# LayerNorm of the first four tiles by ScalarE's square root, x0 loaded in two halves, later loads reordered, and the last tile cut into 512 and 128 columns

## The chip, the cores and the metric

The kernel runs on one core of one Trainium2 chip. The metric is the device time of one execution in microseconds (us). The core has five engines with instruction streams of their own: TensorE (PE; its weight loads are shown apart as PEld), VectorE (DVE), ScalarE (ACT), GpSimd (POOL) and SyncE (SP). ScalarE, GpSimd and SyncE also issue DMAs, each into a queue of its own, and 16 DMA engines carry them all.

## The reference

The input x has 2048 rows of 640 numbers. It is normalized per row, and two branches of the normalized rows are added to x: a sliding, dilated local attention with 32 heads of 20 columns and 8 positions, and a bilinear gated unit.

```python
def _layernorm(x, axis=-1, eps=1e-5):
    m = jnp.mean(x, axis=axis, keepdims=True)
    v = jnp.var(x, axis=axis, keepdims=True)
    return (x - m) / jnp.sqrt(v + eps)

def _A_ref(x, wqkv, wo):          # H = 32, Dh = 20, W, dil = 8, 2
    qkv = (x @ wqkv).reshape(B, S, 3, H, Dh).transpose(2, 0, 3, 1, 4)
    idx = pos[:, None] - (jnp.arange(W) * dil)[None, :]
    ...
    logits = jnp.einsum("bhsd,bhswd->bhsw", q, kg) * scale   # -1e9 where idx < 0
    o = jnp.einsum("bhsw,bhswd->bhsd", softmax(logits), vg)
    return o.transpose(0, 2, 1, 3).reshape(B, S, D) @ wo

def _B_ref(x, w_gate, w_up, w_down):     # F = 1536
    return ((x @ w_gate) * (x @ w_up)) @ w_down

xn = _layernorm(x)
return x + _A_ref(xn, A_wqkv, A_wo) + _B_ref(xn, B_w_gate, B_w_up, B_w_down)
```

All inputs and the output are bfloat16.

## The kernel before

The 2048 rows are 16 tiles of 128 rows (t = 0 to 15), four tiles to a chunk of 512 rows (c = 0 to 3). For a tile the kernel loads x (line 166), takes its statistics in two halves of 320 columns (L251), joins them to mean and variance (L257), adds eps (L259), raises to the power -0.5 on GpSimd (L265), and subtracts and multiplies in place (L270). The normalized tile is transposed into xnT, in tiles 0 to 3 by TensorE against an identity (L345), three blocks of 128 columns and then two, each with a copy out of PSUM (L351); from tile 4 on by a DMA transpose issued on SP (L339). TensorE then makes, by chunk, q and k (L407), by tile v in two halves of 320 columns (L440), the logits from VectorE's products of q and shifted k (L478, L488), gate and up (L614), and by tile the down projection together with the attention's output projection, into one PSUM group of 320 columns at a time (L652, L655). VectorE adds x (L661), and the tile is stored (L683; the last two tiles from SP). v goes through a DRAM buffer vD (L461), from which the shifted rows are gathered.

The order of the instructions is a planner's. Each piece of work is a `Step` with an engine, a cost, a shorter time for which it holds the engine (`occ`), and the steps that it needs. `Plan.order` gives every step a latest time (`late`, from its successors) and then plays the engines forward in time, taking on each engine, of the steps that are ready, the one with the earliest `late`. The engines run the instructions in the order so found; the chip's semaphores then decide when each one starts. What is fixed by hand: `inline` chains VectorE's steps of the first tiles one behind another, `pe_main` chains TensorE's main stream and makes it wait for one of six PSUM banks, `load` chains the loads of SP's queue and gives each an assumed landing (`floor`), and `behind(s, a)` makes step s come after step a.

At the start ScalarE's queue issues the two halves of wv (after VectorE's memset of one of its elements, L192) and then loads the table for Exp with a dummy activation (L177); SP's queue issues x0 to x3, then wq (behind a like memset), x4, wk, and x5 to x7 as tiles 0 to 2 have been transposed, since x has five buffers. TensorE runs ten matmuls on zeros (L242) before the first transposes, so that its clock is up. Tile 0 is normalized in two pieces, 384 and 256 columns, and the second copy of its transposes is VectorE's; the others are ScalarE's.

Of the kernel before, what the change touches and what calls it, by code (L numbers as in the profile page):

```python
# [31 lines left out]
class Plan:  # L32
# [15 lines left out]
    def order(self):  # L48
        for s in self.steps:
            s.left = len(s.deps)  # L50
            for d in s.deps:
                d.succ.append(s)
        for s in reversed(self.steps):
            s.late = min([t.late for t in s.succ], default=0.0) - s.cost
        for s in self.steps:
            if s.urgent:
                s.late = -1e6 + s.idx
        free = {}
        queue = {}
        ready = {}  # L60
        for s in self.steps:
            if s.left == 0:
                ready.setdefault(s.eng, []).append((0.0, s))
        out = []
        while True:
            best = None
            for eng, items in ready.items():
                if not items:
                    continue
                f = free.get(eng, 0.0)  # L70
                t0 = max(f, min(r for r, _ in items))
# [12 lines left out]
            out.append(s)  # L84
            for t in s.succ:
                t.left -= 1
                if t.left == 0:
                    at = max(
                        d.start + d.occ if d in t.after else (d.start + d.occ if d.eng == t.eng and d.eng in self.INORDER else d.end + (0.0 if d.eng == t.eng else self.LAG) + t.margin)
                        for d in t.deps  # L90
                    )
                    ready.setdefault(t.eng, []).append((at, t))
        assert len(out) == len(self.steps)
        return out
# [3 lines left out]
def kernel(  # L98
# [11 lines left out]
    nc = tc.nc  # L110
# [35 lines left out]
    wd = const.tile([P, FT, D], BF, name="wd")  # L146
    ident = const.tile([P, P], BF, name="ident")
    mhalf = const.tile([P, 1], F32, name="mhalf")
    Ek = const.tile([P, KT, H], BF, name="Ek")
    negm = const.tile([P, 2, HALO], F32, name="negm")  # L150
    vD = dram.tile([HALO + S, D], BF, name="vD")
# [11 lines left out]
    def load_x(t, eng=None):  # L163
# [2 lines left out]
            (eng or nc.sync).dma_start(out=x[:], in_=x_flat[t * P : (t + 1) * P, :])  # L166
        return fn

    X = {}

    def wload(dst, src, eng=None):
        return lambda: (eng or nc.sync).dma_start(out=dst[:], in_=src.rearrange("(i p) f -> p i f", p=P))

    def table():
        dm = sb.tile([P, 1], F32, name="dm", tag="dm")
        nc.vector.memset(dm[:], 0.0)
        nc.scalar.activation(dm[:], dm[:], ACT.Exp)  # L177

    chain = [None]
    WL = {}  # L180
# [10 lines left out]
    def hold(dst):  # L191
        return lambda: nc.vector.memset(dst[0:1, 0, 0:2], 0.0)  # L192

    X[0] = load(3.0, load_x(0))
    X[1] = load(3.8, load_x(1))
    X[2] = load(4.9, load_x(2))
    X[3] = load(5.3, load_x(3))

    def consts0():
        wz = new("wz", [P, CS], BF, "gs", 3)  # L200
        nc.vector.memset(wz[:], 0.0)  # L201
        hold(wv)()
        nc.vector.memset(mhalf[:], -0.5)
        make_identity(nc, ident[:])

    def consts_e():
# [26 lines left out]
    C0 = add("POOL", 0.6, consts0)  # L233
    WV = [add("ACT", 4.6, part(0), [C0], occ=0.45)]
    WV.append(add("ACT", 5.6, part(1), occ=0.45, after=[WV[0]]))
    TB = add("ACT", 1.6, table, after=[WV[1]])
    CZ = add("POOL", 3.0, consts_z, [C0], occ=1.2)

    def warm():
        ps = psum.tile([P, 512], F32, name="ps", tag="ps", bufs=6)  # L240
        for _ in range(10):
            nc.tensor.matmul(ps[:], lhsT=T["wz"][:, 0:P], rhs=T["wz"][:], start=True, stop=True)  # L242

    main = add("PE", 4.4, warm, [C0])


    def ln_stats(t, g):
# [6 lines left out]
    def ln_aggr(t):  # L254
        def fn():
            mv = new(("mv", t), [P, nc.vector.BN_AGGR_DIM], F32, "mv", 6)
            nc.vector.bn_aggr(mv[:], T["st", t][:])  # L257
            ve = new(("ve", t), [P, 1], F32, "ve", 6)
            nc.vector.tensor_scalar(ve[:], mv[:, 1:2], scalar1=EPS, scalar2=None, op0=ALU.add)  # L259
        return fn  # L260
# [17 lines left out]
    def behind(s, a):  # L278
        s.after.append(a)
        s.deps.append(a)  # L280
        plan.steps.remove(s)
        plan.steps.append(s)

    def inline(eng, cost, fn, deps=(), occ=None):
        s = line[eng] = add(eng, cost, fn, deps, occ=occ, after=[line.get(eng)])
        return s

    def st_in(t, g, d=None):
        return inline("DVE", 0.48, ln_stats(t, g), [d or X[t]], 0.395)

    def aggr_in(t, d):
        GL[t] = inline("DVE", 0.39, ln_aggr(t), [d], 0.35)
        RS[t] = add("POOL", 0.56, ln_rstd(t), [GL[t]])

    def apply_in(t):
        XT[t] = inline("DVE", 0.443, ln_apply(t), [RS[t]], 0.4)
# [24 lines left out]
    def transposes(t):  # L321
# [19 lines left out]
        def half(g0, g1, n):  # L341
            def pe():
                ps = new(("pst", t, n), [P, KT, P], BF, "ps", 6, psum)
                for g in range(g0, g1):
                    nc.tensor.transpose(ps[:, g, :], T["x", t][:, g * P : (g + 1) * P], ident[:])  # L345

            def ev():
                if n == 0:
                    slot()
                o, i = T["xnT", c][:, g0:g1, q * P : (q + 1) * P], T["pst", t, n][:, g0:g1, :]  # L350
                nc.scalar.copy(o, i) if t or n == 0 else nc.vector.tensor_copy(o, i)  # L351
            return pe, ev

        if t < CH:
# [3 lines left out]
            TX[t] = add("ACT", 0.5, ea, [a], occ=0.42)  # L358
            ring.append(TX[t])
            a = pe_main(0.11, pb, [XT[t]])  # L360
            if t:
                TT[t] = add("ACT", 0.42, eb, [a, TX[t]], occ=0.33)
                behind(VE[t - 1][0], TT[t])
            else:
                TT[t] = inline("DVE", 0.4, eb, [a], 0.33)
            ring.append(TT[t])
        elif t < XDMA:
            a = pe_main(0.28, pe, [XT[t]])
# [5 lines left out]
            else:  # L374
                a = TT[t] = add("SP", 2.8, dma, [XT[t], GP.get(c - 2)], occ=1.28, kb=200)
        if t + 5 < W:
            X[t + 5] = load(11.9 + 0.45 * t, load_x(t + 5), [a])
        elif t == 3:
            X[t + 5] = add("ACT", 6.0, load_x(t + 5, nc.scalar), [a], occ=0.45)
        elif 8 <= t < NT - 5:  # L380
# [136 lines left out]
    def softmax(c, hf):  # L517
# [13 lines left out]
        def ex():  # L531
            nc.scalar.activation(T["d", n][:], T["d", n][:], ACT.Exp, scale=scale)

        e = add("ACT", 0.635, ex, [DD[n]], occ=0.54)
        e.margin = 0.8

        def nrm():
# [104 lines left out]
    def down(t):  # L642
        c, q = divmod(t, CH)
        load_xr(t)
        evs = []
        def pe(n, f0, f1, wo_part):
            if f0 == 0:
                new(("psD", t, n), [P, 512], F32, "ps", 6, psum)
            ps = T["psD", t, n]
            sl = slice(n * NS, (n + 1) * NS)  # L650
            for f in range(f0, f1):
                nc.tensor.matmul(ps[:, 0:NS], lhsT=T["hT", c, f][:, q * P : (q + 1) * P], rhs=wd[:, f, sl],  # L652
                                 start=(f == 0), stop=(f == FT - 1 and not wo_part))
            for g in range(KT if wo_part else 0):
                nc.tensor.matmul(ps[:, 0:NS], lhsT=T["oT", t][:, g, :], rhs=wo[:, g, sl],  # L655
                                 start=False, stop=(g == KT - 1 and f1 == FT))

        def evict(n, a):
            def ev():
                sl = slice(n * NS, (n + 1) * NS)  # L660
                nc.vector.tensor_tensor(T["xr", t][:, sl], T["psD", t, n][:, 0:NS], T["xr", t][:, sl], ALU.add)  # L661
            e = add("DVE", 0.486, ev, [a, XR[t]], occ=0.4)
            ring.append(e)
            evs.append(e)

# [9 lines left out]
            a = ends[1]  # L675
        else:
            for n in range(2):
                a = pe_main((FT + KT) * 0.136, lambda n=n: pe(n, 0, FT, True), [*hs, *W2])
                evict(n, a)
        DT[t] = a  # L680

        def st():
            (nc.sync if t >= NT - 2 else nc.gpsimd).dma_start(out=out_flat[t * P : (t + 1) * P, :], in_=T["xr", t][:])  # L683

        OB[t] = add("SP" if t >= NT - 2 else "POOL", 2.3, st, evs, occ=0.5)


    a = st_in(0, 0)
    a = st_in(0, 1, a)
    HQ = inline("DVE", 0.08, hold(wq))  # L690
    aggr_in(0, a)
    WQ = load(8.8, wload(wq, A_wqkv[:, 0:D]), [HQ])
    X[4] = load(9.2, load_x(4))
    WK = load(11.4, wload(wk, A_wqkv[:, D : 2 * D]))
    a = st_in(1, 0)
    a = st_in(1, 1, a)
    XT[0, 0] = inline("DVE", 0.31, ln_apply(0, 0, 3 * P), [RS[0]], 0.25)
    XT[0, 1] = inline("DVE", 0.26, ln_apply(0, 3 * P, D), [RS[0]], 0.2)
    XT[0] = XT[0, 1]
    aggr_in(1, a)  # L700
    halo(0)
    transposes(0)
    vproj(0, (0,))
    a = st_in(2, 0)
    apply_in(1)
    transposes(1)
    a = st_in(2, 1, a)
    aggr_in(2, a)
    vproj(0, (1,))
    vproj(1, (0,))  # L710
    a = st_in(3, 0)
    a = st_in(3, 1, a)
    apply_in(2)
    transposes(2)
    aggr_in(3, a)
    behind(VS[0], RS[3])
    vproj(1, (1,))
    vproj(2, (0,))
    apply_in(3)
    transposes(3)  # L720
    vproj(2, (1,))
# [7 lines left out]
        X[t] = load(30.0, load_x(t), [TT[t - 5]])  # L729
    WL["u"] = load(36.0, wload(wu, B_w_up))  # L730
    qk(0, 0, CS)
    vproj(3)

    def between(c, work):
# [66 lines left out]
```

## Time and profile before

| what | value |
|---|---|
| time, median of 3 runs | 266.16 us (266.08 to 266.64) |
| the profiled execution: its time, its span | 266.25 us, 264.5 us |
| busy: PE, DVE, ACT, POOL | 98%, 81%, 40%, 15% of the span |
| first and last matmul of the span | 1.27 us, 260.88 us |
| loads: 160 KB for a tile of x, 400 KB for half of wv, 800 KB for wq and for wk | |

The span is the time from the first to the last instruction in the profile; the execution's own time lies around it. In the order of time a row shows the start, the duration, the engine, the line, the operation, the tiles written and read, the shapes, how many instructions are merged (x10), and in brackets the idle time before with what ended it. A row with a "q" behind the engine (SPq) is the issue of a DMA. In a table of windows each engine's busy time stands with its number of instructions in the order PE, PEld, DVE, ACT, POOL, and then the granted clock, the busy share of the DMA engines, and GB/s. Durations of matmuls are pipelined: of several in a row, the pitch from start to start is what each one costs.

### The profile page before, as it was taken

How to read it: one execution, taken by the hardware profiler on the slowest of the kernel's cores; microseconds unless marked ns; L12 is line 12 of the kernel's file. 1: busy time of each engine (PE TensorE's matmuls, PEld its weight loads, DVE VectorE, ACT ScalarE, POOL GpSimd, SP SyncE). 2: the span in 40 equal slices, each digit the busy share in tenths (PEclk: the TensorE clock that was granted, in tenths of full speed). 3: DMA queues.
4: the chain of work that ended last, by engine and by line, in shares of the span. 5: the costliest groups of instructions: out<-in, count | busy, mean ns of one | idle time of the engine just before them, and what ended most of it. 6: DMA issues, size and time to landing. Idle time of an engine off the chain costs nothing.

```text
span 264.5 us, 4077 instructions
## 1 busy us (share of the span) xinstructions
PE 258.5 (98%) x1556; PEld 140.8 (53%) x1574; DVE 215.5 (81%) x338; ACT 106.5 (40%) x196; POOL 40.7 (15%) x84
## 2 busy tenths in 40 slices
PE   7999999999999999999999999999999999999994
PEld 2645445444676546444466754644447764445773
DVE  5785998999999999999994799999938999951221
ACT  2655556655300166555510135555552005554000
POOL 4541027000021221400001000410000104000000
PEclk9999999999999999999999999999999999999999
DMA  7968996999994194983142767891109467110001
GB/s 222 372 131 244 401 341 173 369 289 255 351 239 108 35 318 146 264 290 90 25 99 72 243 223 126 235 312 25 22 15 304 151 185 214 25 25 0 27 25 50
DMA packets 50563, 46.55 MB, mean 176 GB/s; under 512 B 24642, under 2 KB 47696, under 8 KB 50544
## 3 DMA queue, kind: packets, MB, share of 16 engines
q1 hardware_dynamic: 46704, 37.26, 49.7%
q0 software_dynamic: 2384, 8.05, 8.7%
q10 hardware_dynamic: 1456, 0.98, 1.2%
q8 instruction: 12, 0.20, 0.3%
q14 instruction: 7, 0.06, 0.1%
HBM read 35.39 MB, written 5.26 MB: 154 GB/s over the span
## 4 chain that ended last, share of the span: by engine, by line
PE 97%; DVE 1%; issue 0%
PE ps L614 39%; PE ps L652 20%; PE ps L407 16%; PE ps L655 8%; PE ps L440 7%; PE pl L488 4%; PE ps L242 2%; DVE st L251 1%; PE ps L345 1%; DVE x L270 0%; DVE xr L661 0%; DVE xnT L351 0%; DVE gs L201 0%; DVE mv L257 0%; DVE ve L259 0%
## 5 line engine op out<-in xcount | busy, mean ns | idle before, releaser
L614 PE MATMUL ps<-xnT,wg 128*128 128x512 bf16 x227 | 59.0, 379 | 0.7
L614 PE MATMUL ps<-xnT,wu 128*128 128x512 bf16 x240 | 59.6, 379 | 0.0
L652 PE MATMUL ps<-wd,hT 128*128 128x320 bf16 x384 | 57.4, 299 | 0.0
L478 DVE TENSOR_TENSOR pw<-q,k 128x2560 bf16<-128x2560 bf16 x32 | 46.4, 1484 | 3.2 <-ACT k L414 2.4
L652 PEld LDWEIGHTS <-hT 128*128 128x128 bf16 x384 | 37.3, 98 | 16.3 <-issue 1.3
L575 DVE TENSOR_TENSOR v<-v,a 128x5120 bf16<-128x5120 bf16 x16 | 45.1, 2818 | 0.0
L619 ACT CAST gs<-ps 128x512 bf16<-128x512 f32 x48 | 28.1, 586 | 37.6 <-PE ps L614 37.6
L614 PEld LDWEIGHTS <-wu 128*128 128x128 bf16 x240 | 23.5, 98 | 28.3
L614 PEld LDWEIGHTS <-wg 128*128 128x128 bf16 x240 | 23.3, 98 | 28.1 <-issue 0.8
L619 ACT CAST us<-ps 128x512 bf16<-128x512 f32 x48 | 28.1, 586 | 23.3 <-PE ps L614 23.3
L661 DVE TENSOR_TENSOR xr<-ps,xr 128x320 bf16<-128x320 f32 x32 | 14.9, 484 | 19.0 <-PE ps L655 15.7
L630 DVE TENSOR_TENSOR hT<-gs,us 128x512 bf16<-128x512 bf16 x48 | 19.6, 419 | 12.6 <-ACT us L619 12.5
L683 POOL DMA_DIRECT2D out_dram<-xr x14 | 7.6, 545 | 129.2 <-DVE xr L661 129.2
L655 PE MATMUL ps<-wo,oT 128*128 128x320 bf16 x160 | 27.0, 299 | 0.0
L584 DVE TENSOR_TENSOR v<-v 128x2560 bf16<-128x2560 bf16 x16 | 23.8, 1485 | 0.1
L440 PE MATMUL ps<-wv,xnT 128*128 128x320 bf16 x160 | 23.2, 299 | 0.4 <-ACT xnT L351 0.4
L407 PE MATMUL ps<-xnT,wk 128*128 128x512 bf16 x99 | 22.4, 379 | 0.1
L407 PE MATMUL ps<-xnT,wq 128*128 128x512 bf16 x96 | 22.0, 379 | 0.2
L440 PEld LDWEIGHTS <-xnT 128*128 128x128 bf16 x160 | 15.3, 98 | 7.5 <-ACT xnT L351 0.6
L655 PEld LDWEIGHTS <-oT 128*128 128x128 bf16 x160 | 15.7, 98 | 6.1
L501 ACT CAST L<-pl 128x512 bf16<-128x512 f32 x8 | 4.7, 586 | 34.2 <-PE pl L488 32.0
L414 ACT CAST q<-ps 128x512 bf16<-128x512 f32 x20 | 11.7, 586 | 13.0 <-PE ps L407 13.0
(55 smaller groups left out, 188.9 us busy)
## 6 DMA issues: line engine op xcount, KB each, us to landing
v<-vD SPq DMA_DIRECT2D x16, 1280.0 KB, 7.5
vD<-v_t POOLq DMA_DIRECT2D x16, 160.0 KB, 3.1
xr<-in_A_x_dram POOLq DMA_DIRECT2D x16, 160.0 KB, 6.0
out_dram<-xr POOLq DMA_DIRECT2D x14, 160.0 KB, 2.2
x<-in_A_x_dram SPq DMA_DIRECT2D x12, 160.0 KB, 5.8
wg<-in_B_w_gate_dram SPq DMA_DIRECT2D x1, 1920.0 KB, 7.8
wu<-in_B_w_up_dram SPq DMA_DIRECT2D x1, 1920.0 KB, 12.0
wd<-in_B_w_down_dram SPq DMA_DIRECT2D x1, 1920.0 KB, 15.0
```

The costliest lines, as they stand in the source:

```text
L407: nc.tensor.matmul(T[key][:, 0:n], lhsT=(wk if r else wq)[:, i, j * P : (j + 1) * P], rhs=T["xnT", c][:, i, lo : lo + n], start=(i == 0), ...
L414: nc.scalar.copy(dst, T[key][:, 0:n])
L440: nc.tensor.matmul(T["psv", t, n][:, 0:NS], lhsT=T["xnT", c][:, i, q * P : (q + 1) * P], rhs=wv[:, i, n * NS : (n + 1) * NS], start=(i == ...
L478: nc.vector.tensor_tensor(p[:], T["q", c][:], T["k", c][:, :, DIL * i : DIL * i + CS], ALU.mult)
L575: nc.vector.tensor_tensor(v[:].rearrange("p w (j h) -> p w j h", j=Dh, h=H), v[:].rearrange("p w (j h) -> p w j h", j=Dh, h=H), T["a", n][ ...
L584: nc.vector.tensor_tensor(v[:, 0:4, :], v[:, 0:4, :], v[:, 4:8, :], ALU.add)
L614: nc.tensor.matmul(ps[:], lhsT=(wu if r else wg)[:, i, f * P : (f + 1) * P], rhs=T["xnT", c][:, i, :], start=(i == 0), stop=(i == KT - 1))
L619: nc.scalar.copy(s[:], T[key][:])
L630: nc.vector.tensor_tensor(h[:], T["gs", c, f][:], T["us", c, f][:], ALU.mult)
L652: nc.tensor.matmul(ps[:, 0:NS], lhsT=T["hT", c, f][:, q * P : (q + 1) * P], rhs=wd[:, f, sl], start=(f == 0), stop=(f == FT - 1 and not wo ...
L655: nc.tensor.matmul(ps[:, 0:NS], lhsT=T["oT", t][:, g, :], rhs=wo[:, g, sl], start=False, stop=(g == KT - 1 and f1 == FT))
L661: nc.vector.tensor_tensor(T["xr", t][:, sl], T["psD", t, n][:, 0:NS], T["xr", t][:, sl], ALU.add)
```

## The change

For tiles 0 to 3 the variance goes to ScalarE, which takes the square root with eps as its bias, and VectorE takes the reciprocal; the eps add on VectorE and the power on GpSimd go. ScalarE loads the table for Sqrt at the start, and the one for Exp after the second eviction of q of chunk 0. The loads change: x0 comes in two halves of 64 rows from SP and ScalarE, x3 from ScalarE behind wv, wq after x0 is normalized, wk behind x4, x5 and x6. VectorE's order of the first tiles is changed, the second copy of tile 0's transposes goes to ScalarE, and each Sqrt stands in front of the second copy of the tile before. There are nine matmuls on zeros for ten. The last tile's output is made, added and stored as 512 and 128 columns for twice 320. In the planner `late` is computed in an order of the graph, for reversed order of the list, in which a step that was given a later dependency could be reached too early.

```diff
-        for s in reversed(self.steps):
+        todo = {s: len(s.succ) for s in self.steps}
+        work = [s for s in self.steps if not s.succ]
+        while work:
+            s = work.pop()
             s.late = min([t.late for t in s.succ], default=0.0) - s.cost
+            for d in s.deps:
+                todo[d] -= 1
+                if not todo[d]:
+                    work.append(d)
...
+    def load_x0(eng, lo, hi):
+        def fn():
+            if ("x", 0) not in T:
+                new(("x", 0), [P, D], BF, "x", 5)
+            eng.dma_start(out=T["x", 0][lo:hi, :], in_=x_flat[lo:hi, :])
+        return fn
...
-    X[0] = load(3.0, load_x(0))
+    X[0] = load(2.9, load_x0(nc.sync, 0, P // 2))
+    X0 = add("ACT", 2.9, load_x0(nc.scalar, P // 2, P), occ=0.3)
     X[1] = load(3.8, load_x(1))
     X[2] = load(4.9, load_x(2))
-    X[3] = load(5.3, load_x(3))
...
-    TB = add("ACT", 1.6, table, after=[WV[1]])
+    X[3] = add("ACT", 5.0, load_x(3, nc.scalar), occ=0.45, after=[WV[1]])
+    TB = add("ACT", 1.6, table(ACT.Sqrt), after=[X[3]])
...
-        for _ in range(10):
+        for _ in range(9):
...
+            if t < CH:
+                return
             ve = new(("ve", t), [P, 1], F32, "ve", 6)
             nc.vector.tensor_scalar(ve[:], mv[:, 1:2], scalar1=EPS, scalar2=None, op0=ALU.add)
...
+    def ln_std(t):
+        def fn():
+            nc.scalar.activation(new(("std", t), [P, 1], F32, "ve", 6)[:], T["mv", t][:, 1:2], ACT.Sqrt, bias=epst[:])
+        return fn
+
+    def ln_inv(t):
+        return lambda: nc.vector.reciprocal(new(("rstd", t), [P, 1], F32, "rstd", 6)[:], T["std", t][:])
...
-        RS[t] = add("POOL", 0.56, ln_rstd(t), [GL[t]])
+        RS[t] = add("ACT", 0.24, ln_std(t), [GL[t], TB], occ=0.2)
+
+    def inv_in(t):
+        RS[t] = inline("DVE", 0.15, ln_inv(t), [RS[t]], 0.12)
...
-                nc.scalar.copy(o, i) if t or n == 0 else nc.vector.tensor_copy(o, i)
+                nc.scalar.copy(o, i)
...
+        last = t == NT - 1
+        at = [0, 512, D] if last else [0, NS, D]
...
-        OB[t] = add("SP" if t >= NT - 2 else "POOL", 2.3, st, evs, occ=0.5)
+        if last:
+            for n in range(2):
+                add("SP", 2.1, lambda n=n: st(at[n], at[n + 1]), [evs[n]], occ=0.5)
+        else:
+            OB[t] = add("SP" if t >= NT - 2 else "POOL", 2.3, st, evs, occ=0.5)
...
     a = st_in(0, 1, a)
+    aggr_in(0, a)
+    a = st_in(1, 0)
+    inv_in(0)
+    XT[0, 0] = inline("DVE", 0.31, ln_apply(0, 0, 3 * P), [RS[0]], 0.25)
+    XT[0] = XT[0, 1] = inline("DVE", 0.26, ln_apply(0, 3 * P, D), [RS[0]], 0.2)
     HQ = inline("DVE", 0.08, hold(wq))
-    aggr_in(0, a)
-    WQ = load(8.8, wload(wq, A_wqkv[:, 0:D]), [HQ])
-    X[4] = load(9.2, load_x(4))
-    WK = load(11.4, wload(wk, A_wqkv[:, D : 2 * D]))
-    a = st_in(1, 0)
     a = st_in(1, 1, a)
-    XT[0, 0] = inline("DVE", 0.31, ln_apply(0, 0, 3 * P), [RS[0]], 0.25)
-    XT[0, 1] = inline("DVE", 0.26, ln_apply(0, 3 * P, D), [RS[0]], 0.2)
-    XT[0] = XT[0, 1]
+    WQ = load(10.0, wload(wq, A_wqkv[:, 0:D]), [HQ])
+    X[4] = load(10.5, load_x(4))
     aggr_in(1, a)
     halo(0)
     transposes(0)
+    behind(TT[0], RS[1])
     vproj(0, (0,))
     a = st_in(2, 0)
+    inv_in(1)
     apply_in(1)
     transposes(1)
+    WK = load(13.6, wload(wk, A_wqkv[:, D : 2 * D]))
     a = st_in(2, 1, a)
     aggr_in(2, a)
+    behind(TT[1], RS[2])
...
     qk(0, 0, CS)
+    TE = add("ACT", 1.6, table(ACT.Exp), [Q[0][1]], occ=1.5)
```

Tiles 2 and 3 follow in the same pattern: the first half of the next tile's statistics, the reciprocal, the apply, the second half.

More of the change, by code (lines that the diff above doesn't have):

```diff
@@ L148 @@
     mhalf = const.tile([P, 1], F32, name="mhalf")
+    epst = const.tile([P, 1], F32, name="epst")
     Ek = const.tile([P, KT, H], BF, name="Ek")
@@ L172, in wload, with table @@
         return lambda: (eng or nc.sync).dma_start(out=dst[:], in_=src.rearrange("(i p) f -> p i f", p=P))
[L174 to L177, printed above, removed]
+    def table(f):
+        def fn():
+            if "dm" not in T:
+                nc.vector.memset(new("dm", [P, 1], F32, "dm", 1)[:], 0.0)
+            nc.scalar.activation(T["dm"][:], T["dm"][:], f)
+        return fn
     chain = [None]
@@ L203, in consts0 @@
         nc.vector.memset(mhalf[:], -0.5)
+        nc.vector.memset(epst[:], EPS)
         make_identity(nc, ident[:])
@@ L240, in warm @@
         ps = psum.tile([P, 512], F32, name="ps", tag="ps", bufs=6)
-        for _ in range(10):
+        for _ in range(9):
             nc.tensor.matmul(ps[:], lhsT=T["wz"][:, 0:P], rhs=T["wz"][:], start=True, stop=True)
-    main = add("PE", 4.4, warm, [C0])
+    main = add("PE", 4.0, warm, [C0])
     def ln_stats(t, g):
@@ L280, in behind @@
         s.deps.append(a)
-        plan.steps.remove(s)
-        plan.steps.append(s)
     def inline(eng, cost, fn, deps=(), occ=None):
@@ L288, in st_in, with fn @@
     def st_in(t, g, d=None):
-        return inline("DVE", 0.48, ln_stats(t, g), [d or X[t]], 0.395)
+        return inline("DVE", 0.48, ln_stats(t, g), d if isinstance(d, list) else [d or X[t]], 0.395)
+    def ln_std(t):
+        def fn():
+            nc.scalar.activation(new(("std", t), [P, 1], F32, "ve", 6)[:], T["mv", t][:, 1:2], ACT.Sqrt, bias=epst[:])
+        return fn
+    def ln_inv(t):
+        return lambda: nc.vector.reciprocal(new(("rstd", t), [P, 1], F32, "rstd", 6)[:], T["std", t][:])
     def aggr_in(t, d):
-        GL[t] = inline("DVE", 0.39, ln_aggr(t), [d], 0.35)
-        RS[t] = add("POOL", 0.56, ln_rstd(t), [GL[t]])
+        GL[t] = inline("DVE", 0.28, ln_aggr(t), [d], 0.24)
+        RS[t] = add("ACT", 0.24, ln_std(t), [GL[t], TB], occ=0.2)
+    def inv_in(t):
+        RS[t] = inline("DVE", 0.15, ln_inv(t), [RS[t]], 0.12)
     def apply_in(t):
@@ L360, in transposes @@
             a = pe_main(0.11, pb, [XT[t]])
+            TT[t] = add("ACT", 0.42, eb, [a, TX[t]], occ=0.33)
             if t:
-                TT[t] = add("ACT", 0.42, eb, [a, TX[t]], occ=0.33)
                 behind(VE[t - 1][0], TT[t])
-            else:
-                TT[t] = inline("DVE", 0.4, eb, [a], 0.33)
             ring.append(TT[t])
@@ L376, in transposes @@
         if t + 5 < W:
-            X[t + 5] = load(11.9 + 0.45 * t, load_x(t + 5), [a])
+            X[t + 5] = load((11.0, 11.5, 14.2)[t], load_x(t + 5), [a])
         elif t == 3:
@@ L532, in ex @@
             nc.scalar.activation(T["d", n][:], T["d", n][:], ACT.Exp, scale=scale)
-        e = add("ACT", 0.635, ex, [DD[n]], occ=0.54)
+        e = add("ACT", 0.635, ex, [DD[n], TE], occ=0.54)
         e.margin = 0.8
@@ L648, in pe @@
                 new(("psD", t, n), [P, 512], F32, "ps", 6, psum)
-            ps = T["psD", t, n]
-            sl = slice(n * NS, (n + 1) * NS)
+            sl = slice(at[n], at[n + 1])
+            ps = T["psD", t, n][:, 0 : at[n + 1] - at[n]]
             for f in range(f0, f1):
-                nc.tensor.matmul(ps[:, 0:NS], lhsT=T["hT", c, f][:, q * P : (q + 1) * P], rhs=wd[:, f, sl],
+                nc.tensor.matmul(ps, lhsT=T["hT", c, f][:, q * P : (q + 1) * P], rhs=wd[:, f, sl],
                                  start=(f == 0), stop=(f == FT - 1 and not wo_part))
             for g in range(KT if wo_part else 0):
-                nc.tensor.matmul(ps[:, 0:NS], lhsT=T["oT", t][:, g, :], rhs=wo[:, g, sl],
+                nc.tensor.matmul(ps, lhsT=T["oT", t][:, g, :], rhs=wo[:, g, sl],
                                  start=False, stop=(g == KT - 1 and f1 == FT))
@@ L659, in ev @@
             def ev():
-                sl = slice(n * NS, (n + 1) * NS)
-                nc.vector.tensor_tensor(T["xr", t][:, sl], T["psD", t, n][:, 0:NS], T["xr", t][:, sl], ALU.add)
-            e = add("DVE", 0.486, ev, [a, XR[t]], occ=0.4)
+                w = at[n + 1] - at[n]
+                sl = slice(at[n], at[n + 1])
+                nc.vector.tensor_tensor(T["xr", t][:, sl], T["psD", t, n][:, 0:w], T["xr", t][:, sl], ALU.add)
+            cost = 0.153 + (at[n + 1] - at[n]) / 960
+            e = add("DVE", cost, ev, [a, XR[t]], occ=cost - 0.08)
             ring.append(e)
@@ L677, in down, with st @@
             for n in range(2):
-                a = pe_main((FT + KT) * 0.136, lambda n=n: pe(n, 0, FT, True), [*hs, *W2])
+                a = pe_main((FT + KT) * ((at[n + 1] - at[n]) / 2400 + 0.003), lambda n=n: pe(n, 0, FT, True), [*hs, *W2])
                 evict(n, a)
         DT[t] = a
-        def st():
-            (nc.sync if t >= NT - 2 else nc.gpsimd).dma_start(out=out_flat[t * P : (t + 1) * P, :], in_=T["xr", t][:])
-        OB[t] = add("SP" if t >= NT - 2 else "POOL", 2.3, st, evs, occ=0.5)
-    a = st_in(0, 0)
-    a = st_in(0, 1, a)
-    HQ = inline("DVE", 0.08, hold(wq))
-    aggr_in(0, a)
-    WQ = load(8.8, wload(wq, A_wqkv[:, 0:D]), [HQ])
-    X[4] = load(9.2, load_x(4))
-    WK = load(11.4, wload(wk, A_wqkv[:, D : 2 * D]))
-    a = st_in(1, 0)
+        def st(lo=0, hi=D):
+            e = nc.sync if t >= NT - 2 else nc.gpsimd
+            e.dma_start(out=out_flat[t * P : (t + 1) * P, lo:hi], in_=T["xr", t][:, lo:hi])
+        if last:
[3 more added lines that the diff above has]
+            OB[t] = add("SP" if t >= NT - 2 else "POOL", 2.3, st, evs, occ=0.5)
+    a = st_in(0, 0, [X[0], X0])
+    a = st_in(0, 1, a)
+    aggr_in(0, a)
[3 more added lines that the diff above has]
+    XT[0] = XT[0, 1] = inline("DVE", 0.26, ln_apply(0, 3 * P, D), [RS[0]], 0.2)
+    HQ = inline("DVE", 0.08, hold(wq))
     a = st_in(1, 1, a)
-    XT[0, 0] = inline("DVE", 0.31, ln_apply(0, 0, 3 * P), [RS[0]], 0.25)
-    XT[0, 1] = inline("DVE", 0.26, ln_apply(0, 3 * P, D), [RS[0]], 0.2)
-    XT[0] = XT[0, 1]
+    WQ = load(10.0, wload(wq, A_wqkv[:, 0:D]), [HQ])
+    X[4] = load(10.5, load_x(4))
     aggr_in(1, a)
@@ L711 @@
     a = st_in(3, 0)
-    a = st_in(3, 1, a)
+    inv_in(2)
     apply_in(2)
     transposes(2)
+    a = st_in(3, 1, a)
     aggr_in(3, a)
-    behind(VS[0], RS[3])
+    behind(TT[2], RS[3])
     vproj(1, (1,))
     vproj(2, (0,))
+    inv_in(3)
     apply_in(3)
```

## The prediction

> **What bounds the kernel now.** I read the page first (shares, chain), then the start in order of time, then the DMA landings, then the end.
>
> ```profile
> PE   7999999999999999999999999999999999999994
> ...
> PE 97%; DVE 1%; issue 0%
> ```
>
> TensorE is the chain: 97% of it, short only in the first and the last slice. From the third group of transposes (9.51 us) to the last matmul (260.88) I find no wait of PE in the trace, so the time between is fixed work, and a change can act only before 9.51, after 260.88, or by bringing a stall in between. The start, in order of time:
>
> ```profile
> 1.27 4.45 PE L242 MATMUL ps<-gs 128*128 128x512 bf16 x10 [1.27 <-DVE wv L192]
> ...
> 2.34 1.28 ACT L177 ACT_TABLE_LOAD   x1 [2.34 <-issue]
> 3.63 0.20 ACT L177 ACTIVATE dm<-dm 128x1 f32<-128x1 f32 x1
> ...
> 4.65 0.57 POOL L265 TENSOR_TENSOR rstd<-ve,mhalf 128x1 f32<-128x1 f32 x1 [1.70 <-DVE ve L259]
> ...
> 5.27 0.62 DVE L270 TENSOR_SCALAR x<-x,mv,rstd 128x384 bf16<-128x384 bf16 x2
> 5.69 0.72 PE L345 MATMUL ps<-ident,x 128*128 128x128 bf16 x5
> 6.23 0.48 ACT L351 COPY xnT<-ps 128x384 bf16<-128x384 bf16 x1 [2.39 <-PE ps L345]
> ...
> 6.65 0.48 DVE L251 BATCH_NORM_STATS2 st<-x 128x6 f32<-128x320 bf16 x1
> ...
> 7.05 0.43 DVE L270 TENSOR_SCALAR x<-x,mv,rstd 128x640 bf16<-128x640 bf16 x1
> ...
> 7.54 0.45 PE L345 MATMUL ps<-ident,x 128*128 128x128 bf16 x5
> ...
> 9.51 0.45 PE L345 MATMUL ps<-ident,x 128*128 128x128 bf16 x5
> ```
>
> Call the four groups of transposes T0 to T3: 5.69, 7.54, 9.51, 11.16. Between T0 and T2 PE should need 5 transposes x 2 + 15 v matmuls, 0.56 + 2.04 = 2.60 us at full clock, but takes 3.82: 1.2 us are waits for LayerNorm and evictions (and half clock, see the rivals). Each normalization passes VectorE (statistics, +eps), GpSimd (power, 0.55 us) and VectorE again.
>
> The transfers of the same stretch, as busy time by engine in one window and as landings after issue:
>
> ```profile
> 3.12:6.53 3.41, 3.28 (x12) 1.04 (x9) 2.94 (x12) 1.01 (x3) 0.82 (x2) 1.00 1.07 338
> ```
>
> ```profile
> x<-in_A_x_dram SPq DMA_DIRECT2D x1, 160.0 KB, 4.7
> ...
> wv<-in_A_wqkv_dram ACTq DMA_DIRECT2D x1, 400.0 KB, 6.1
> ```
>
> The DMA share is full (1.07, 338 GB/s). x2, issued at 1.74, lands at 6.4; the second half of wv, issued at 1.76, at 7.88. In the same way x0 lands at 3.21, x1 at 4.10, x3 at 7.21, wq (issued 4.17) at 10.15, wk at 12.88. The end:
>
> ```profile
> 260.33 0.84 PE L655 MATMUL ps<-wo,oT 128*128 128x320 bf16 x5
> 261.21 0.49 DVE L661 TENSOR_TENSOR xr<-ps,xr 128x320 bf16<-128x320 f32 x1 [1.82 <-PE ps L655]
> 261.73 0.35 SPq L683 DMA_DIRECT2D out_dram<-xr  x1
> ```
>
> The last eviction (0.49), its store (landing 1.79 after the issue) and 1.02 us of closing semaphores follow the last matmul one by one.
>
> **The change, the start.** I carry the changed order of each engine forward with these durations and the gaps of the trace (0.05 us engine to engine, 0.035 within VectorE).
>
> x0 in halves: I take nothing for it, x0 at 3.21 as now; bounds: 0.2 earlier (the second issue of 0.40 us runs beside the first) to 0.1 later. The Trainium skill (DMA: Bandwidth & Descriptors, Rules for kernel authors) advises against two transfers to disjoint partition halves, since they share the same 16 engines and serialize. By that rule this edit gains zero, which is what I sum.
>
> ScalarE: the extra x0 issue fits before 1.27, where wv waits for VectorE's memset anyway; x3's issue (0.43) comes ahead of the table load, which so ends at 2.78 + 1.28 = 4.06, and its dummy at 4.27. The mean and variance of x0 are ready at 4.37, so the table is 0.15 us early. Sqrt on 128x1 starts 4.42; nothing shows it, the dummy activation of one column took 0.20, the 128x256 copy 0.38; I take 0.23, near the first. VectorE meanwhile does half of x1's statistics (till 4.76); the reciprocal of one column lies between the 128x1 add (0.15) and the 128x64 reciprocal (0.55); I take 0.15, as 63 of 64 columns are gone. It ends at 4.86, apply 4.90 to 5.26, T0 at 5.32: 0.37 earlier. Nine warm matmuls end at 1.27 + 9 x 0.427 = 5.11; the tenth would have held PE till 5.54.
>
> Then: T0's third transpose (half clock) ends 5.82, its copy 5.86 to 6.34. The Sqrt of x1 is queued behind that copy though its input is ready at 6.24, and the second copy of T0, moved here from VectorE, behind the Sqrt: 6.34 to 6.57, then to 6.88, and v's last two matmuls of tile 0 end at 7.2. VectorE's statistics of x2 stand ahead of x1's reciprocal, so x2's landing enters. Its queue has 80 KB less ahead of it: 80 / 338 = 0.24 us, 6.15 for 6.39 (bounds: 6.39, and 6.0, below which the Sqrt decides). Reciprocal 6.62, apply 6.80 to 7.23, T1 7.29 for 7.54. V's second half (0.28 later, 7.57) needs wv's second half, now at 7.88; x3 (160 KB, 0.47 us at that rate) has left its competitor queue, so about 7.4.
>
> T2: copy of T1 7.66 to 8.14, Sqrt of x2 behind it to 8.28, reciprocal 8.33 to 8.48, apply 8.52 to 8.95, T2 9.01, against PE free at 7.57 + 1.36 = 8.93. In the same way T3 at 10.72 for 11.16 (Sqrt of x3 behind T2's copy, 9.77 to 9.99). After T3 PE is gapless again: **start -0.44** (bounds -0.22 with x2 at 6.39, -0.55 with x0 0.1 earlier and so T0).
>
> What it moves: x3 behind wv on ScalarE's queue is needed at 7.78 to 7.88 and lands at about 7.7 if the engines stay as busy (all of x0 to x3 and wv were in by 7.88, part of wq included). wq is issued at about 5.57 for 4.17, after the memset that VectorE now does after x0's apply; its bytes still follow the same 1440 KB, so it lands at 10.15 to 10.5, needed at 11.7. wk goes behind x4 to x6, 320 KB or 0.9 us more: 13.8, needed at 17.1. x5 and x6 land about 2 us sooner, so their normalization and SP's transposes (the last landing at 23.35, needed at 24.27) move ahead with PE. GpSimd loses four powers of 0.55; the power of x4 goes behind the constants (about 2 us), ready near 12.9, and apply of x4 (14.12 now, held by x5's landing) is no later. The second table load (1.28 + 0.20) falls between the evictions of q; ScalarE idles 0.49 before each of them, so it is caught up after four, and six banks (about 5 us of matmuls) cover it: 0; uncovered it would be 1.5.
>
> The middle: the latest times are now computed over the whole graph, which puts the logits of one group after 10 v matmuls for 15 and the next group after four GLU groups (about 47.0) for 80.6. VectorE must have four products of chunk 1 by then; its fourth would end near 46.06 less the 0.4 that the start moves, 1.3 us in time. The softmax of chunk 0 comes one product (1.48) later; o of tile 3 came at 78.2, its matmuls at 86: covered. 0.
>
> **The end.** The last tile's 34 matmuls of 320 columns take 34 x 0.136 = 4.62; 17 of 512 and 17 of 128 take 17 x 0.216 + 17 x 0.056 (the pitch of the warm transposes, same shape) = 4.62: 0. Upper bound: each weight load of 98 ns unhidden, 17 x 0.042 = +0.71. The 512-column eviction (0.49 + 192/0.96 ns = 0.69) starts at 260.26, ends at 260.95, and its store is issued by 261.33. The last eviction has 128 columns: 0.49 - 0.20 = 0.29. The last store of 256-byte rows is taken as the present one, 1.79; bounds -0.15 and +0.4 (no store of that row in the trace). **End -0.20.**
>
> Sum -0.64. The profiled execution took 266.25 (span 264.5, 1.7 around it): 265.61. It stands 0.09 over the median, 266.16; against the median 265.5.
>
> **Rivals.** (1) The new order makes a transfer the bound: x3, behind 800 KB of wv and beside wq's larger packets, or wv's second half, lands at 8.3 or later. For: every engine is full, and 7.7 is only 0.1 early. Against: wq starts later. Price: the statistics of x3 stand ahead of x2's reciprocal, so T2 goes to 9.4 and T3 to 11.1: start -0.05, in all 265.9. (2) The clock opens later: slower. The trace's clock record grants the full clock from 6.53; before it 512 columns take 0.427, after 0.216. With nine warm matmuls PE pauses at 5.11, 5.74 and till 6.39, and in the 3.4 us before 6.53 it is fed for 2.7 instead of 2.9. If that is below what opens it, T1, the next ten v matmuls and T2 run at half rate: 0.25 + 10 x 0.13 from T1 at 7.4, T2 at 10.3, T3 at 11.95: +0.8 - 0.2, 266.75. It decides only if the clock is still half at 7.5. The Trainium skill (TensorE: Matmul & The Clock Gate, Part 1: The HAM clock gate) says that a free-running window of 3413 ns decides by how busy PE was. The trace agrees on the window: full clock held 259.41 us, 76.0 of them; the next would open at 9.94. (3) The small matmuls or the small store eat the end: +0.5 there with the start kept, 266.2.
>
> **How the numbers follow.** Forecast 0.56; transfer 0.22; clock 0.11; end 0.07; a stall of 0.5 or so in the middle 0.04. About 0.2% (0.53 us: 265.63 and 266.69) is what a measurement of this kernel can tell. Faster: the forecast and a little of the first rival, 0.59; same: 0.28 (rivals 1 and 3); slower: 0.13. Range: -0.55 and -0.35 (short store, x0 early) with a margin, 265.1, up to 266.6, leaving out most of the clock's case.
>
> **What would show it.** T0 to T3 at 5.3, 7.3, 9.0, 10.7; the Sqrt (about 0.23) right behind each copy; x3 by 7.9, wq by 10.6; PE without a wait from T3 on; the last eviction 0.29 and its store landing 1.8 after the issue. T3 after 11.0, a wait of PE for a weight, or 128-column matmuls over 0.06 apart would make it wrong.

## The result, and the profile after

The changed kernel takes 267.97 us (median of 5, 267.75 to 269.43), the kernel before 266.16 (median of 5, 265.97 to 266.64). The ratio is 1.0082, with a 95% interval of 1.0060 to 1.0104: slower, where 265.5 was forecast. The profiled execution took 267.75 us, with a span of 266.0.

The page of the changed kernel, PE's busy time and clock in 40 slices, and the chain:

```profile
PE   5999999999999999999999999999999999999995
...
PEclk9799999999999999999999999999999999999999
...
PE 96%; DMA 2%; DVE 0%; SPq 0%; ACT 0%; issue 0%
```

PE's first digit is 5 where it was 7, the clock is 7 in the second slice, and a DMA now has 2% of the chain. The start of the changed kernel in order of time:

```profile
0.80 0.59 SPq L181 DMA_DIRECT2D x<-in_A_x_dram  x1
0.80 0.55 ACTq L181 DMA_DIRECT2D x<-in_A_x_dram  x1
...
4.72 0.29 ACT L312 ACTIVATE ve<-mv,epst 128x1 f32<-128x1 f32 x1
5.84 0.49 DVE L270 BATCH_NORM_STATS2 st<-x 128x6 f32<-128x320 bf16 x1 [1.15 <-DMA x<-in_A_x_dram]
6.25 0.15 DVE L316 RECIPROCAL rstd<-ve 128x1 f32<-128x1 f32 x1
6.43 0.64 DVE L291 TENSOR_SCALAR x<-x,mv,rstd 128x384 bf16<-128x384 bf16 x2
6.87 0.54 PE L375 MATMUL ps<-ident,x 128*128 128x128 bf16 x5 [2.03 <-DVE x L291]
...
9.09 0.74 PE L375 MATMUL ps<-ident,x 128*128 128x128 bf16 x5
...
11.70 0.44 PE L375 MATMUL ps<-ident,x 128*128 128x128 bf16 x5
...
13.48 0.45 PE L375 MATMUL ps<-ident,x 128*128 128x128 bf16 x5
```

T0 to T3 are at 6.87, 9.09, 11.70 and 13.48 (before: 5.69, 7.54, 9.51, 11.16). The Sqrt of x0 is done at 5.01, but its reciprocal comes at 6.25: VectorE's order has the first half of x1's statistics in front of it, and VectorE waits 1.15 us for x1. The landings after the issue show x1 (issued at 1.44) at 5.8, against 4.10 before:

```profile
x<-in_A_x_dram SPq DMA_DIRECT2D x1, 160.0 KB, 4.4
```

PE has been idle for 2.03 us before T0, and soon after the granted clock falls to half. The window from 7.70 to 11.10 (clock third from the end):

```profile
7.70:11.10 3.40, 3.32 (x16) 2.12 (x17) 2.66 (x10) 1.84 (x7) 0.00 (x0) 0.50 0.77 246
```

From T3 to the last matmul it is 249.62 us (249.72 before), so no stall was brought into the middle. The end is shorter:

```profile
262.88 0.44 PE L686 MATMUL ps<-wo,oT 128*128 128x128 bf16 x5
...
263.36 0.29 DVE L693 TENSOR_TENSOR xr<-ps,xr 128x128 bf16<-128x128 f32 x1 [0.26 <-PE ps L686]
263.68 0.33 SPq L717 DMA_DIRECT2D out_dram<-xr  x1
```

From the start of the last matmul (263.10) to the end of the span it is 2.95 us, before 3.66.

So the start lost 13.48 - 11.16 = 2.32 us, the middle gave 0.10, the end 0.71: 1.5 us in the spans (266.05 for 264.54) and between the two profiled executions (267.75 for 266.25).

### The profile page after: what moved, and what is told of

Read it like the earlier page. It is cut to its first block, busy times and chain, and to the rows that moved or that the text cites. A ratio compares the mean times of both kernels' runs of the same rounds, so it can differ in the third digit from the quotient of the medians.

```text
span 266.0 us, 4104 instructions
## 1 busy us (share of the span) xinstructions
PE 259.7 (98%) x1573; PEld 140.2 (53%) x1573; DVE 215.6 (81%) x338; ACT 108.7 (41%) x203; POOL 37.7 (14%) x80
## 4 chain that ended last, share of the span: by engine, by line
PE 96%; DMA 2%; DVE 0%; SPq 0%; ACT 0%; issue 0%
PE ps L642 39%; PE ps L683 20%; PE ps L435 16%; PE ps L468 9%; PE ps L686 8%; PE pl L516 4%; DMA x<-in_A_x_dram 2%; PE ps L375 1%; SPq L181 0%; DVE st L270 0%; ACT xnT L381 0%; DVE x L291 0%; DVE xr L693 0%; DVE rstd L316 0%
## 5 line engine op out<-in xcount | busy, mean ns | idle before, releaser
L642 PE MATMUL ps<-xnT,wg 128*128 128x512 bf16 x240 | 59.7, 379 | 0.0
L683 PE MATMUL ps<-wd,hT 128*128 128x320 bf16 (+2 forms) x384 | 57.4, 299 | 0.0
L693 DVE TENSOR_TENSOR xr<-ps,xr 128x320 bf16<-128x320 f32 (+2 forms) x32 | 14.9, 485 | 18.8 <-PE ps L686 15.5
L686 PE MATMUL ps<-wo,oT 128*128 128x320 bf16 (+2 forms) x160 | 27.0, 299 | 0.0
L468 PE MATMUL ps<-wv,xnT 128*128 128x320 bf16 x160 | 24.6, 311 | 0.4 <-ACT xnT L381 0.4
L270 DVE BATCH_NORM_STATS2 st<-x 128x6 f32<-128x320 bf16 x32 | 14.1, 479 | 3.4 <-DMA x<-in_A_x_dram 3.4
```

Of the source, the lines that this page charges most:

```text
L270: nc.vector.bn_stats(T["st", t][:, g, :], T["x", t][:, g * NS : (g + 1) * NS])
L468: nc.tensor.matmul(T["psv", t, n][:, 0:NS], lhsT=T["xnT", c][:, i, q * P : (q + 1) * P], rhs=wv[:, i, n * NS : (n + 1) * NS], start=(i == ...
L642: nc.tensor.matmul(ps[:], lhsT=(wu if r else wg)[:, i, f * P : (f + 1) * P], rhs=T["xnT", c][:, i, :], start=(i == 0), stop=(i == KT - 1))
L683: nc.tensor.matmul(ps, lhsT=T["hT", c, f][:, q * P : (q + 1) * P], rhs=wd[:, f, sl], start=(f == 0), stop=(f == FT - 1 and not wo_part))
L686: nc.tensor.matmul(ps, lhsT=T["oT", t][:, g, :], rhs=wo[:, g, sl], start=False, stop=(g == KT - 1 and f1 == FT))
```

## The experiments

All times are medians; each ratio is to the kernel before, run on the same chip. In several of these kernels single executions lie up to 1.9 us apart. The windows of TensorE's clock fall at another place in each profiled execution (the first full clock on record starts at 4.26 us in the changed kernel, 4.86 with x1's statistics moved, 5.92 with the halves alone, 6.53 before), which may be the reason; where it matters, the text says what the profiled execution shows.

**x0's halves alone, in the kernel before.** Theory Q: the halves put x1's issue behind wv's first half, and x1 lands behind its 400 KB. Rival S: ScalarE's longer list (issues, table, Sqrt) makes the start late. This kernel has no Sqrt.

```diff
-    X[0] = load(3.0, load_x(0))
+    def load_x0():
+        x, h = new(("x", 0), [P, D], BF, "x", 5), P // 2
+        nc.sync.dma_start(out=x[0:h, :], in_=x_flat[0:h, :])
+        nc.scalar.dma_start(out=x[h:P, :], in_=x_flat[h:P, :])
+    X[0] = load(3.0, load_x0)
```

> The kernel before with x0 in two halves from SP and ScalarE and nothing else. Theory Q: x1 lands near 5.8; both halves of its statistics stand ahead of x0's apply here, so T0 comes at about 7.1 (5.69 before) and T3 1.4 to 2.4 later than 11.16: 267.5 to 268.5 us. Rival S: x1 does not matter, 266.2 us.

Measured: 268.42 us, ratio 1.0076 (1.0059 to 1.0093). Its start:

```profile
5.78 0.89 DVE L256 BATCH_NORM_STATS2 st<-x 128x6 f32<-128x320 bf16 x2 [0.91 <-DMA x<-in_A_x_dram]
6.59 0.62 DVE L275 TENSOR_SCALAR x<-x,mv,rstd 128x384 bf16<-128x384 bf16 x2
7.01 0.54 PE L350 MATMUL ps<-ident,x 128*128 128x128 bf16 x5 [1.29 <-DVE x L275]
```

The same wait for x1, landing at 5.76, and T0 at 7.01. The halves by themselves cost 268.42 - 266.14 = 2.3 us; S falls.

**The whole change, without the halves.**

```diff
-    X[0] = load(2.9, load_x0(nc.sync, 0, P // 2))
-    X0 = add("ACT", 2.9, load_x0(nc.scalar, P // 2, P), occ=0.3)
+    X[0] = load(2.9, load_x(0))
...
-    a = st_in(0, 0, [X[0], X0])
+    a = st_in(0, 0)
```

> The changed kernel with x0 in one transfer from SP again; all else of the change kept. Theory Q (the halves put x1's issue behind that of wv's first half, so x1 lands 1.7 us late and holds the reciprocal of x0 on VectorE): x1 lands at about 4.1, T0 at 5.4, T3 at 10.8 to 11.0, the clock does not fall back to half, the end as in the changed kernel (0.75 shorter): 265.1 us. Rival S (the way over ScalarE, with Sqrt behind the table load and behind copies, is itself slower than the power): T0 and T3 stay late by 1 to 2 us, 267.0 to 268.0.

Measured: 265.13 us, ratio 0.9962 (0.9950 to 0.9974). Its transposes in order of time:

```profile
5.28 0.71 PE L374 MATMUL ps<-ident,x 128*128 128x128 bf16 x5
...
7.23 0.45 PE L374 MATMUL ps<-ident,x 128*128 128x128 bf16 x5
...
9.01 0.45 PE L374 MATMUL ps<-ident,x 128*128 128x128 bf16 x5
...
10.80 0.45 PE L374 MATMUL ps<-ident,x 128*128 128x128 bf16 x5
```

These are the forecast 5.32, 7.29, 9.01 and 10.72 to within 0.08 us. All else in the change is worth -1.0 us; the halves cost 267.97 - 265.13 = 2.8.

**x1's statistics behind the apply of x0.** The halves stay; the order that the planner found is kept but for one step.

```diff
-    a = st_in(1, 0)
+    S10 = a = st_in(1, 0)
...
-    for s in plan.order():
+    steps = plan.order()
+    steps.remove(S10)
+    steps.insert(steps.index(HQ) + 1, S10)
+    for s in steps:
```

> The changed kernel, halves kept, with one instruction moved: the first half of x1's statistics after the apply of x0 on VectorE. Theory Q: x1 still lands near 5.8, but T0 no longer waits for it and comes at 5.4; T1 waits for x1 and comes near 7.9, T3 near 11.6; full clock from T1 on; start +0.4, end -0.75: 265.8 us. Rival S: T0 stays near 6.9 and the time at 267.5 to 268.

Measured: 267.28 us, ratio 1.0032 (1.0017 to 1.0047), from 265.90 to 267.81. The first transposes of the profiled execution (267.30):

```profile
5.59 0.54 PE L375 MATMUL ps<-ident,x 128*128 128x128 bf16 x5 [0.46 <-DVE x L291]
5.74 0.89 DVE L270 BATCH_NORM_STATS2 st<-x 128x6 f32<-128x320 bf16 x2
```

T0 (5.59), T1 (8.04) and x1's landing (5.72) are near what Q expected. T3 (13.02) and the time are not: Q expected full clock from T1 on, and the granted clock is half from 8.27 to 11.69. The six executions with a mean granted clock of 0.994, which one such window makes, took 267.30 to 267.81 us; the six with 1.000 took 265.90 to 267.27. So x1 is late in itself, and its place ahead of the reciprocal made T0 1.28 us later (6.87 - 5.59).

**18 warm matmuls for 9**, in the changed kernel, to keep PE fed while it waits for x1 (`range(9)` to `range(18)`).

> The changed kernel with 18 warm matmuls and not 9, so that TensorE has work until about 6.8 while it waits for x0's transposes; nothing else. Theory K (the late x1 costs twice: once as a wait, T0 at 6.87, and once more because the pause of 2.0 us lets the granted clock fall to half for 3.41 us): T0 stays at 6.87, the clock stays full, T0 to T3 takes 5.6 and not 6.6, time 266.8 to 267.1. Rival L (the wait alone; the clock is not tied to the pause): T0 to T3 stays 6.6, 267.9 or so.

Measured: 267.48 us, ratio 1.0042 (1.0030 to 1.0055); the profiled execution took 266.80. Its clock in the same window as above:

```profile
7.70:11.10 3.40, 3.14 (x26) 1.75 (x27) 3.14 (x10) 2.34 (x8) 0.00 (x0) 1.00 0.77 227
```

T0 is at 7.04, and T0 to T3 takes 5.49 us for 6.61: K holds in this execution, and there the half clock is worth 1.1 us. The other executions took 267.3 to 267.7, above what K expected, and what they lost isn't known, since they have no profile.

**The start's edits without the last tile's, and the last tile's alone.** First the kernel with x0 whole and `last = False`; then the kernel before with only the last tile as 512 and 128.

> The changed kernel with x0 whole and with the last tile in two equal columns again: the start's edits alone (Sqrt and reciprocal, x3, wq and wk moved). If start and end add up: 265.13 + 0.60 (the last tile alone gave 266.14 - 265.56 = 0.58) = 265.7, T0 to T3 as with x0 whole (5.28 to 10.80), the end as before (last matmul to end 3.66). If the two overlap (the last tile's gain depends on the start or on the clock's windows): 265.3 or 266.1.

> The kernel before with the last tile as 512 and 128 columns and nothing else. From the two traces (from the last matmul's start to the end of the span 3.66 and 2.92): 0.75 shorter, 265.4 us. By the sum of the prediction (only the eviction shorter): 0.2 shorter, 265.95 us.

Measured: 265.75 us, ratio 0.9982 (0.9974 to 0.9990), and 265.56, ratio 0.9977 (0.9968 to 0.9986). Together 0.51 + 0.58 = 1.09 below the kernels before, and the kernel with both is 1.01 below: they add up. The last tile alone is worth 0.58 us (in its trace the last matmul to the end takes 3.01 us for 3.66), much nearer to the 0.71 of the changed kernel's trace than to the forecast's 0.20.

**wv a little later.** Why is x1 late? If its place behind wv's issue decides, a small delay of wv should free it.

```diff
+        nc.vector.memset(wd[:, 0, 0:CS], 0.0)
         hold(wv)()
```

> The changed kernel with x0 still in two halves; one more memset of 128x512 on VectorE stands ahead of the one that lets wv go, so wv's first half is issued about 0.2 us behind x1 and not 0.05 us ahead of it. Theory Q (x1 is late because wv's 400 KB are queued ahead of it): x1 lands at 4.0 to 4.3 again and not at 5.81, wv's first half at about 6.3; T0 5.3 to 5.7, T3 11.0 to 11.4 (V of tile 0 waits a little for wv); with the tail's -0.7 the time is 265.3 to 265.7. Rival H (two half issues at once hold up whatever is issued next, in any order): x1 lands at 5.3 or later, T0 above 6.3, 267 or more.

Measured: 268.05 us, ratio 1.0068 (1.0053 to 1.0083). The two issues, ScalarE's and SP's:

```profile
1.45 0.80 SPq L174 DMA_DIRECT2D x<-in_A_x_dram  x1
...
1.51 0.48 ACTq L206 DMA_DIRECT2D wv<-in_A_wqkv_dram  x1
```

wv is issued after x1 now, and yet x1 lands at 5.89, which is what H expected. Q isn't out, since x1's issue is 0.80 long (0.41 before) and still ends after wv's. Q in the form "the issue that ends later waits" is called Q2 from here on. Three kernels tell the two apart.

**wv later still** (two larger memsets, 2048 columns in all, in the same place).

> The changed kernel with x0 in halves; two more memsets on VectorE (into a weight's buffer that is loaded much later) let wv go some 0.6 us later, so that its first half is issued at about 1.9, when x1's issue of 1.44 should be over. The run with a shift of 0.1 us left two readings. Q2: x1 is late because it is issued in the same half microsecond as wv's 400 KB, on the other queue, and gets its rows moved behind wv's; then x1's issue takes 0.4 and not 0.8, its first packets move at 2.5 to 2.9 and not 3.6, it lands at 4.0 to 4.3; T0 5.4 to 5.7, V of tile 0 waits for wv (landing 6.3 to 6.7), T3 11.1 to 11.5, time 265.4 to 265.9. H: the two half issues at 0.80 hold up the next issue on SP whatever else is issued: x1's issue takes 0.8 again, it lands at 5.4 or later, time 267.5 or more.

Measured: 267.12 us, ratio 1.0021 (1.0006 to 1.0036), from 266.04 (profiled) to 267.45. x1's issue and wv's, and x1's landing after its issue:

```profile
1.44 0.81 SPq L174 DMA_DIRECT2D x<-in_A_x_dram  x1
...
2.32 0.43 ACTq L206 DMA_DIRECT2D wv<-in_A_wqkv_dram  x1
```

```profile
x<-in_A_x_dram SPq DMA_DIRECT2D x1, 160.0 KB, 3.0
```

With wv's issue (2.32) after the end of x1's (2.25), x1 lands at 4.40, close to Q2 and not to H. But its issue takes 0.81 us again, though wv's issue starts only behind it: that part is as H expected. T0 came only at 6.29, and so the time missed both: wv's later issue also pushed ScalarE's table load back, to 3.94, and the Sqrt to 5.34. What was tried to free x1 made ScalarE late.

**Both halves from SP.** `X0 = load(2.9, load_x0(nc.sync, P // 2, P))`.

> The changed kernel with both halves of x0 issued by SP, one behind the other, and none by ScalarE; so no two issues start at 0.80, but x1's comes at about 1.6, after wv's first half (1.25). Q2 (behind wv's issue on the other queue): x1 lands at 5.5 or later, T0 above 6.5, time 267.5 or more. H (only two half issues at once do it): x1 lands at 4.2 to 4.6, T0 5.4 to 5.7, time 265.2 to 265.7.

Measured: 269.19 us, ratio 1.0109 (1.0092 to 1.0125); T0 at 7.75. ScalarE's and SP's issues:

```profile
1.25 0.44 ACTq L206 DMA_DIRECT2D wv<-in_A_wqkv_dram  x1
1.46 0.57 SPq L181 DMA_DIRECT2D x<-in_A_x_dram  x1
...
2.07 0.59 SPq L174 DMA_DIRECT2D x<-in_A_x_dram  x1
```

Now x0's second half, whose issue ends after wv's, lands behind wv's first half (5.21 after 5.02), and x1 at 6.70. Q2 expected this; H expected x1 at 4.2 to 4.6.

**x1 from ScalarE, ahead of wv.** `X[1] = add("ACT", 3.0, load_x(1, nc.scalar), occ=0.45, after=[X0])`, and wv behind it.

> The changed kernel with x0 in halves as they are; x1 is issued by ScalarE right behind its half of x0 and ahead of wv's first half, on the same queue; x2 takes x1's place on SP. Q2: x1's rows come ahead of wv's, it lands at 4.0 to 4.4, wv's first half at 6.3 to 6.7, x2 by 7.2; T0 5.4 to 5.7, T3 11.1 to 11.5, time 265.3 to 265.9, no better than x0 whole (265.13). H: x1 lands at 5.4 or later here too, time 267.5 or more.

Measured: 267.17 us, ratio 1.0035 (1.0021 to 1.0048). x1 lands at 3.93 and wv's first half at 6.78, close to Q2; the time missed. T0 is at 6.00, since the table load stands behind one more issue (3.66, the Sqrt at 5.06), and in the profiled execution the full clock starts only at 10.32.

**x0 in two parts by columns**: 128 rows of 320, still from SP and ScalarE.

```diff
-            eng.dma_start(out=T["x", 0][lo:hi, :], in_=x_flat[lo:hi, :])
+            eng.dma_start(out=T["x", 0][:, lo:hi], in_=x_flat[0:P, lo:hi])
...
-    X[0] = load(2.9, load_x0(nc.sync, 0, P // 2))
-    X0 = add("ACT", 2.9, load_x0(nc.scalar, P // 2, P), occ=0.3)
+    X[0] = load(2.9, load_x0(nc.sync, 0, NS))
+    X0 = add("ACT", 2.9, load_x0(nc.scalar, NS, D), occ=0.3)
```

> The changed kernel with x0 still in two parts from SP and ScalarE, but cut by columns: 128 rows of 320 columns each, for 64 rows of 640. In all kernels with parts of 64 rows these two issues took 0.55 to 0.60 us (0.40 for the whole of 128 rows) and SP's next issue took 0.57 to 0.82 (0.41 without parts). Reading R (it is the 64 rows): the two issues take 0.40 to 0.45, x1 is issued at about 1.3 in 0.4 us, ends before wv's first half or with it and lands at about 4.0; T0 5.2 to 5.5, time 265.0 to 265.5. Reading C (it is two transfers at once, however cut): the issues take 0.55 or more and x1's 0.8, x1 lands at 5.7 or later, T0 at 6.8 or later, 267.5 or more.

Measured: 265.06 us, ratio 0.9954 (0.9941 to 0.9968). The issues:

```profile
0.80 0.40 SPq L181 DMA_DIRECT2D x<-in_A_x_dram  x1
0.80 0.40 ACTq L181 DMA_DIRECT2D x<-in_A_x_dram  x1
...
1.25 0.45 ACTq L206 DMA_DIRECT2D wv<-in_A_wqkv_dram  x1
1.26 0.41 SPq L174 DMA_DIRECT2D x<-in_A_x_dram  x1
```

Two transfers at once do no harm here: with 128 rows each the issues take 0.40, x1's 0.41, x1 lands at 3.83, T0 is at 5.28. So it is the 64 rows, reading R. The kernel is the fastest measured, and not told apart from x0 whole (265.13).

The issues and landings side by side (us; "ends" is start plus duration of the issue):

| kernel | x1's issue ends | wv's first half: issue ends | x1 lands | wv's first half lands |
|---|---|---|---|---|
| before | 1.28 + 0.41 = 1.69 | 1.73 | 4.10 | 5.15 |
| x0 whole | 1.26 + 0.41 = 1.67 | 1.70 | 3.95 | 6.03 |
| x0 by columns | 1.26 + 0.41 = 1.67 | 1.70 | 3.83 | 5.46 |
| changed | 1.44 + 0.82 = 2.26 | 1.99 | 5.81 | 6.05 |
| wv a little later | 1.45 + 0.80 = 2.25 | 1.99 | 5.89 | 6.14 |
| wv later still | 1.44 + 0.81 = 2.25 | 2.75 | 4.40 | 6.40 |
| x1 from ScalarE | 1.40 + 0.59 = 1.99 | 2.48 | 3.93 | 6.78 |

In every row the transfer whose issue ends first gets its data first; where x1's ends second it lands 1.4 to 2.1 us later than in the other rows. The packets in the traces say so more directly than the landings, since x1 is the smaller transfer and lands first even where it starts second. In the changed kernel wv's first packet moves at 2.74 and x1's first near 3.6; wv later still has x1's near 2.9 and wv's at 3.95. In the two rows where x1 loses, 431 and 425 KB of wv have been started before the last packet of x1; in the other rows it is at most 98 KB. The start of the issue doesn't decide (wv a little later: x1 starts first and loses; before: x1 starts 0.01 later and wins). In the last row both transfers are in ScalarE's queue, so that row says nothing on two queues. What in the chip makes this order is not shown.

## Why the prediction was wrong

**The step that failed is "x0 in halves: I take nothing for it".** It asked only when x0 itself lands, and there its bounds were not far off (halves at 3.11 and 3.46, where 3.01 to 3.31 was allowed). It never asked what the issues do to the next one on SP's queue, and carried x1 on at 4.10: "VectorE meanwhile does half of x1's statistics (till 4.76)". In its place, from the profiled executions (changed 267.75, x0 whole 265.12, 2.63 apart):

- 0.31: x0 lands later, so that T0 is at 5.59 for 5.28 even where nothing of x1 stands ahead (the kernel with x1's statistics moved back: x0's own start at 3.46 for 3.15).
- 1.28: those statistics wait for x1 with the reciprocal behind them, T0 at 6.87.
- 1.09: T0 to T3 takes 6.61 us for 5.52, as PE's pause brings the clock down (5.49 with 18 warm matmuls).

The sum is 2.68, the end gives 0.04 back. It explains the profiled execution, the fastest of five. Two others took 268.75 and 269.43 us with a mean granted clock of 1.000, and what they lost is not shown; the same mean stands at both halves from SP, where the full clock starts only at 13.22 us, so their clock may have opened late.

The Trainium skill (DMA: Bandwidth & Descriptors, Rules for kernel authors) says that two transfers to disjoint partition halves are not worth making, since they serialize. For x0 itself these runs agree that nothing is gained: by halves it is complete at 3.46, whole at 3.13, by columns at 3.30. The prediction read the rule as "zero"; the cost lay in the transfer behind.

**The rest of the start was right.** Without the halves T0 to T3 came as worked out, and from T3 the start gives 0.36 of the forecast's 0.44. The Sqrt took 0.29 for 0.23, the reciprocal 0.15 to 0.17 for 0.15; that T0 came on time all the same is in part luck, as x0 landed at 3.13 for 3.21. The Trainium skill (ScalarE: Activation LUTs, What ACT_TABLE_LOAD costs) gives about 0.28 us for an activation of one column with a pointer as its bias; the trace agrees, and the dummy's 0.20 was the wrong row to size it by. The second table load, x3, wq and wk cost nothing, as forecast: T3 to the last matmul is 249.62 us in the changed kernel and with x0 whole, for 249.72.

**The end was mis-sized.** It was forecast at -0.20, the eviction alone, and the whole end measured -0.71: the eviction 0.20 (0.49 to 0.29), the last matmul's start to the eviction 0.08 (0.34 to 0.26), the store's landing 0.32 (1.79 to 1.46 for 32 KB in rows of 256 bytes), and what follows the landing 0.11 (1.02 to 0.91). The term "taken as the present one" was mis-sized most; its lower bound (-0.15) was too near. The matmuls of 128 columns cost nothing, as forecast. This is most of why the change without the halves gives 1.0 us, not 0.64.

**The rivals.** A transfer did become the bound, but x1, which none of them named. The second rival had the effect, half clock across T1 to T3, with nearly its price (0.8, measured 1.1), but for another cause: not the missing tenth warm matmul (with nine and x0 whole the start is not slowed), but a pause of 2 us behind x1. What it describes, a clock that opens late, did happen with x1 from ScalarE (full clock from 10.32) and with both halves from SP (from 13.22). The rival's 2.9 us of work before 6.53 is not what the row shown for that window has, 3.28. The third was wrong in its sign.

## What to carry to other kernels

When a load is split, look at the issues of the pieces and at the transfer queued behind them, not only at the landing of the load itself; a split that keeps all 128 rows left the neighbours where they were. A chain written in order on an engine turns one late transfer into a wait for everything behind it, here for a tile that had long landed. Size a last store by its own size: its landing, too, was shorter for fewer bytes.

## What was not expected of the hardware

- A load of 64 rows of 1280 bytes took 0.55 to 0.60 us to issue, alone or beside another, and SP's next issue 0.57 to 0.82; a load of 128 rows of 1280 or of 640 bytes took 0.40, and the next 0.41. Why is open.
- Of two loads on SP's and ScalarE's queues whose issues ended within half a microsecond, the one whose issue ended first moved its first packets first (the table); with 0.03 us between the ends the order still held.
- A pause shorter than a window brings the clock down. The full clock held for whole numbers of windows of 3.41 us (259.41 us are 76, 256.0 are 75). By PE's busy time in the window, 1.12 us (changed), 1.50 (wv a little later) and 2.07 (x1's statistics back) were followed by half clock; 1.95 (halves in the kernel before), 2.14 (wv later still), 2.53 (last tile alone) and 3.10 (18 warm matmuls) by full clock. So the boundary lies near 2.0 of 3.41 us here, but busy time alone doesn't set it, as 1.95 kept the clock and 2.07 lost it. To open it took more: windows with 2.29 (both halves from SP) and 2.50 (x1 from ScalarE) were followed by half clock, 2.91 (18 warm matmuls) and 3.01 (changed) by full. The Trainium skill (TensorE: Matmul & The Clock Gate, Part 1: The HAM clock gate) gives the free-running window of 3413 ns, which the trace shows, and an idle window as what ends the full clock; here a window in which PE was busy for 2.07 us ended it.
